# The last pair of output tiles by plain products, and an earlier, fixed order for the pair sums of the last chunk

## The chip, the cores and the metric

The kernel runs on one core of one Trainium2 chip, in one launch. The metric is the device time of an execution in microseconds (us); the lower, the better. Three runs of the kernel before the change took 675.46, 675.48 and 680.38 us, median 675.48.

## The reference

Two stages: a block-sorted attention, and on its output a mixture of 8 experts with a balanced (Sinkhorn) gate. The change lies in the second alone.

```python
def _moe_ref(x, w_gate, w1, w2):          # x 3072x512, w1 8x512x1024, w2 8x1024x512
    logits = x @ w_gate
    P = np.exp(logits - logits.max())
    for _ in range(8):
        P /= P.sum(1, keepdims=True) + 1e-09
        P /= P.sum(0, keepdims=True) + 1e-09
        P *= N / E
    out = np.zeros((N, D), dtype=np.float32)
    for e in range(E):
        h = np.maximum(x @ w1[e], 0.0)
        ye = h @ w2[e]
        out += P[:, e:e + 1] * ye
    return out
```

Every expert is applied to all 3072 rows, and its result is added with the gate's weight of each row.

## The kernel before

The attention and expert 0 come first. Experts 1 to 7 then run over three chunks of 1024 rows each, which makes 21 chunks (`n` from 1 to 21 in the last loop). A chunk has two steps, and the kernel weaves them: while PE (TensorE) does the output products of chunk n, it does the hidden products of chunk n+1 between them (`ahead`, one `next` after each part of an output). Behind chunk 21 there is no hidden work left to weave in.

Hidden step (`hidden`, matmuls at L653): `h = relu(x @ w1)` in transposed form, into a tile `hT` of 128 x 8 x 1024 bf16 (feature within a block, feature block, row of the chunk). Four units i = 0 to 3; unit i makes the blocks i and 4+i. The 2x2 block product is computed by seven block products instead of eight (the Winograd form of Strassen's method). VectorE (L677, L689, L692) and ScalarE (L695) bring the results from PSUM into `hT`; a tile `h3` (L699) gets one of the differences that the output step needs.

Output step (`output7`, matmuls at L740): the chunk's 8 row tiles of 128 rows are taken in four pairs, i = 0 to 3; tile a = 8p + i and tile b = 8p + 4 + i. There are 84 such pairs in the 21 chunks. A pair's product with `w2` is again a 2x2 block product by seven products, each of four matmuls 128x256. It needs three sums of quarters of `hT` (s1, s2, s4), which GpSimd (POOL) makes into a tile `hs` in `sum_h` (L723), and sums of quarters of `w2` (`w2s`), also made by GpSimd. The seven products accumulate into two PSUM tiles, `u` (256 columns) and `x` (512 columns): after some of them the running sum is read by `gather`, and the next product is added to it.

```python
add(u, hT[:, 4:8, ha], b11, True);   gather(e, a, 0, u)
add(x0, hT[:, 0:4, ha], b21, True)
add(u, s2, t2, False);               gather(e, a, 256, u)
add(x1, s1, t1, False);              gather(e, b, 256, x1)
add(u, s3, t3, False);               gather(e, b, 256, u)
add(x1, s4, b22, False);             gather(e, a, 0, x)
add(u, hT[:, 0:4, hb], t4, False);   gather(e, b, 0, u)
```

`gather` (L705) is one VectorE instruction, out = PSUM x gate weight + out, on a float32 accumulator `osbl` in SBUF. For the last expert each finished row tile is stored to DRAM from the SP queue (`store`, L710; for the very last tile b in two halves, L758 and L768).

Order: each engine runs its instructions in the order of its own queue. Instructions that are passed through `pin` keep the order in which the program makes them; the others are placed by a scheduler. `sum_h` isn't pinned before the change. `sum_h(i, hT, f0, f1)` takes the feature blocks f0 to f1 of a quarter. For pair 0 of a chunk it is called twice: for blocks 0 to 2 during the chunk before (128x384 instructions), and for block 3 (128x128) at the chunk's start, as block 3 comes from the last hidden unit. For pair i+1 it is called as a whole (128x512) while pair i is worked on. The pool `hsp` of `hs` tiles has three buffers, PSUM has five banks under the name `bk` and three under `oacc`. In the last chunk the pairs use some `bk` banks for their accumulators too, as the hidden step no longer needs them.

Of the kernel before, what the change touches and what calls it, by code (L numbers as in the profile page):

```python
# [25 lines left out]
def kernel(  # L26
# [11 lines left out]
    nc = tc.nc  # L38
    B, H, S, D = 4, 8, 768, 64
    NB, BL = 8, 96  # L40
    N, Dm, E, F = 3072, 512, 8, 1024
# [22 lines left out]
    pin = tc.keep_in_program_order  # L64
# [12 lines left out]
    w2t = {}  # L77

    def load_w1(e, f0=0, f1=F):
        if e not in w1t:  # L80
            w1t[e] = wp.tile([128, 4, F], BF16, name="w1e")
        pin(nc.gpsimd.dma_start(
            out=w1t[e][:, :, f0:f1],
            in_=moe_w1[e].rearrange("(kk k) f -> k kk f", k=128)[:, :, f0:f1]))

    def load_w2(e):
        w2t[e] = (wq if e else wcp).tile([128, 8, Dm], BF16, name="w2e")
        for f0, f1 in ((0, 8),) if e else ((0, 4), (4, 8)):
            pin(nc.gpsimd.dma_start(
                out=w2t[e][:, f0:f1],  # L90
                in_=moe_w2[e].rearrange("(fb k) f -> k fb f", k=128)[:, f0:f1]))
# [22 lines left out]
    def acc(t, c=0, n=Dm):  # L114
        return osbl[t // 18][:, t % 18, c:c + n]
# [300 lines left out]
    def sum_w(e):  # L416
        wct[e] = (wcq if e % 2 == 0 else wcp).tile([128, 3, 2, F // 2], BF16, name="wc")
        for kk in range(2):
            a11, a21 = (w1t[e][:, kk, f:f + 512] for f in (0, 512))
            a12, a22 = (w1t[e][:, 2 + kk, f:f + 512] for f in (0, 512))  # L420
            s1, s2, s4 = (wct[e][:, j, kk, :] for j in range(3))
            for a, b, o, c in ((a21, a22, ALU.add, s1), (s1, a11, ALU.subtract, s2),
                               (a11, a21, ALU.subtract, a21), (a12, s2, ALU.subtract, s4)):
                pin(nc.gpsimd.tensor_tensor(out=c, in0=a, in1=b, op=o))
                yield

    with tc.tile_pool(name="ps0", bufs=4, space=bass.MemoryType.PSUM,
# [58 lines left out]
        for x in ("s00 k2 s01 k3 p s02 s03 s10 m00 s11 m01 s12 m02 s13 m03 t00 m10 m11 t01 m12 "  # L486
                  "h00 m13 h01 t10 h02 t11 h03 v0 v1 v2 v3 h10").split():
            n = [int(c) for c in x[1:]]
# [29 lines left out]
    with ExitStack() as c2:  # L518
# [53 lines left out]
        for _ in ex:  # L572
# [12 lines left out]
    op = ctx.enter_context(tc.tile_pool(name="op", bufs=3, space=bass.MemoryType.PSUM,  # L585
                                        reuse_waits="tile"))
# [3 lines left out]
    def bank():  # L590
        return bk.tile([128, 512], F32, name="bk")
# [3 lines left out]
    def sum_w2(e):  # L595
        w2s[e] = (w2q.tile([128, 4, 4, Dm // 2], BF16, name="w2s") if e % 2 else
                  wcp.tile([128, 4, 4, Dm // 2], BF16, name="w2e"))
        for k in (0, 2):
            b11, b12 = (w2t[e][:, 4 + k:6 + k, d:d + 256] for d in (0, 256))
            b21, b22 = (w2t[e][:, k:k + 2, d:d + 256] for d in (0, 256))  # L600
            t1, t2, t3, t4 = (w2s[e][:, j, k:k + 2, :] for j in range(4))
            for a, b, c in ((b12, b11, t1), (b22, t1, t2), (b22, b12, t3), (b21, t2, t4)):
                pin(nc.gpsimd.tensor_tensor(out=c, in0=a, in1=b, op=ALU.subtract))
                yield
# [98 lines left out]
    def gather(e, t, c, ps):  # L703
        o = acc(t, c, ps.shape[-1])
        nc.vector.scalar_tensor_tensor(out=o, in0=ps, scalar=glog[:, t, e:e + 1], in1=o,  # L705
                                       op0=ALU.mult, op1=ALU.add)

    def store(e, t):
        if e == E - 1:
            nc.sync.dma_start(out=out[t * 128:(t + 1) * 128, :], in_=acc(t))  # L710

    hs = {}

    def sum_h(i, hT, f0=0, f1=4):

        if f0 == 0:
            hs[i] = hsp.tile([128, 3, 4, 128], BF16, name="hs")
        s1, s2, s4 = (hs[i][:, j, f0:f1] for j in range(3))
        a11, a21, a12, a22 = (hT[:, f + f0:f + f1, t + 128 * i:t + 128 * i + 128]
                              for f in (4, 0) for t in (0, 512))  # L720
        for a, b, o, c in ((a21, a22, ALU.add, s1), (s1, a11, ALU.subtract, s2),
                           (a12, s2, ALU.subtract, s4)):
            nc.gpsimd.tensor_tensor(out=c, in0=a, in1=b, op=o)  # L723

    def output7(e, p, i, hT):
        a, b = 8 * p + i, 8 * p + 4 + i
        ha, hb = slice(128 * i, 128 * i + 128), slice(512 + 128 * i, 640 + 128 * i)
        s1, s2, s4 = (hs[i][:, j] for j in range(3))
        s3 = h3[e, p][:, :, ha]
        t1, t2, t3, t4 = (w2s[e][:, j] for j in range(4))  # L730
        obank = lambda: op.tile([128, Dm], F32, name="oacc")
        last = e == E - 1 and p == 2
        u = (bank if last and i % 2 else obank)()[:, 0:256]
        x = (bank if last and i else obank)()
        x0, x1 = x[:, 0:256], x[:, 256:512]
        b11, b21, b22 = w2t[e][:, 4:8, 0:256], w2t[e][:, 0:4, 0:256], w2t[e][:, 0:4, 256:512]

        def add(ps, h, w, first):
            for fb in range(4):
                nc.tensor.matmul(ps, h[:, fb, :], w[:, fb, :], start=(first and fb == 0),  # L740
                                 stop=(fb == 3), skip_group_check=True)

        add(u, hT[:, 4:8, ha], b11, True)
        gather(e, a, 0, u)
        yield

        add(x0, hT[:, 0:4, ha], b21, True)
        yield
        add(u, s2, t2, False)
        gather(e, a, 256, u)  # L750
        yield
        add(x1, s1, t1, False)
        gather(e, b, 256, x1)
        yield
        add(u, s3, t3, False)
        gather(e, b, 256, u)
        if last and i == 3:
            nc.sync.dma_start(out=out[b * 128:(b + 1) * 128, 256:512],  # L758
                              in_=acc(b, 256, 256))
        yield  # L760
        add(x1, s4, b22, False)
        gather(e, a, 0, x)
        store(e, a)
        yield
        add(u, hT[:, 0:4, hb], t4, False)
        gather(e, b, 0, u)
        if last and i == 3:
            nc.sync.dma_start(out=out[b * 128:(b + 1) * 128, 0:256], in_=acc(b, 0, 256))  # L768
        else:
            store(e, b)  # L770
        yield

    def scale0(ts):
        for t in ts:
            nc.scalar.activation(out=acc(t), in_=acc(t), func=AF.Copy,
                                 scale=glog[:, t, 0:1])
# [7 lines left out]
    def sums(n):  # L784
        while n and queue:
            if next(queue[0], 0) is None:
                n -= 1
            else:
                queue.pop(0)
# [14 lines left out]
    for n in range(56):  # L804
        next(tail0)
        if n == 28:
            hT = htp.tile([128, 8, 1024], BF16, name="hT")
            first = units(1, 0, hT, pin)
        if first:
            next(first)  # L810
            if n == 28 + 21:
                sum_h(0, hT, 0, 3)
        if n in works:
            next(works[n], 0)
        if n in (0, 2, 4, 6, 8, 11, 13, 15, 17, 20, 22, 24, 26, 29, 31, 33, 35, 37, 39):
            next(chain)
        if n == 40:
            pin(nc.gpsimd.tensor_copy(held, glog[0:96, NT - 1, 0:2]))
            sums(8)

    hTs = {0: hT}
# [9 lines left out]
    for n in range(1, 3 * (E - 1) + 1):  # L831
        e, p, hT = 1 + (n - 1) // 3, (n - 1) % 3, hTs[n - 1]
        d = 2 + n // 3
        fetch = n == 1 or n % 3 == 0 and d < E
        if fetch:
            load_w1(d)
            queue.append(sum_w(d))
        for i in range(4):
            if e == 1:
                scale0([t for t in (8 * p + i, 8 * p + 4 + i) if t < 18])  # L840
            if i == 0:
                sum_h(0, hT, 3)
            if i < 3:
                sum_h(i + 1, hT)
            elif n < 3 * (E - 1):
                sum_h(0, hTs[n], 0, 3)
            sums(1 + i // 2)
            for _ in output7(e, p, i, hT):
                next(ahead, 0)
        if fetch:  # L850
            load_w2(d)
            queue.append(sum_w2(d))
# [30 lines left out]
```

## Time and profile before

| What | Value |
|---|---|
| median of 3 runs | 675.48 us |
| the profiled execution's own time | 675.74 us |
| its span, first to last instruction | 673.5 us |
| PE busy | 660.1 us, 98% |
| DVE (VectorE) busy | 544.3 us, 81% |
| POOL (GpSimd) busy | 473.0 us, 70% |
| ACT (ScalarE) busy | 296.1 us, 44% |
| chain that ended last | PE 73%, DVE 1%, POOL 1% |
| L705 gathers into osbl from oacc | 490, mean 521 ns |
| L723 pair sums | 3 x 105, mean 959 ns (all shapes) |

A span is counted from the first to the last instruction of the profiled execution; around it lie 2.2 us of its own time. The profiler's page cuts the span in 40 slices; the views used below (the chain of waits, the timeline of one engine, the stretches) take single microseconds of it, counted from the span's start. A matmul's record is longer than the time to the next one's start, since matmuls are pipelined: the price of one in a stream is read from starts, not from durations.

### The profile page before, as it was taken

The page shows a single profiled execution, that of the slowest core. Times are in us where ns is not written, and L with a number is a line of the kernel's source. Part 1 is how long each engine was busy: PE and PEld are TensorE (multiplying, and loading weights), DVE is VectorE, ACT ScalarE, POOL GpSimd, SP SyncE. Part 2 cuts the span into 40 slices and gives each one's busy share as a digit, 9 for nine tenths or more (in the row PEclk, how much of TensorE's full clock was granted, in tenths as well). Part 3 has the DMA queues.
Part 4 walks back from the last instruction along what each step waited for, and adds up shares of the span by engine and source line. Part 5 has one row for each costly group of instructions (what it writes and reads, how often), then busy time and mean ns, then how long its engine had stood idle before and what let it go on. Part 6 is the DMA issues. An engine that isn't in the chain of part 4 may idle for free.

```text
span 673.5 us, 13293 instructions
## 1 busy us (share of the span) xinstructions
PE 660.1 (98%) x5150; PEld 435.3 (65%) x5150; DVE 544.3 (81%) x1134; ACT 296.1 (44%) x530; POOL 473.0 (70%) x500
## 2 busy tenths in 40 slices
PE   8999999999999999999999999999999999999996
PEld 3656665554666666666666666666666666666675
DVE  6548777663889888888888888988888888888896
ACT  5773863479443434333333334343433334333430
POOL 4713344017897998898897998689886999636745
PEclk9999999999999999999999999999999999999999
DMA  9997964003040340031203040034003220001223
GB/s 158 189 215 133 142 113 64 1 0 54 11 64 6 59 63 1 1 63 29 36 1 63 2 63 1 6 58 63 1 1 65 27 38 1 1 1 62 95 79 142
DMA packets 32800, 36.57 MB, mean 54 GB/s; under 512 B 2097, under 2 KB 25777, under 8 KB 32737
## 3 DMA queue, kind: packets, MB, share of 16 engines
q0 software_dynamic: 26848, 27.57, 26.0%
q1 hardware_dynamic: 5888, 8.15, 3.8%
q8 instruction: 40, 0.66, 0.4%
q14 instruction: 24, 0.19, 0.1%
HBM read 52.45 MB, written 6.29 MB: 87 GB/s over the span
## 4 chain that ended last, share of the span: by engine, by line
PE 73%; DVE 1%; POOL 1%; issue 0%; ACT 0%; DVEq 0%
PE oacc L740 36%; PE bk L653 36%; PE bk L740 1%; DVE osbl L705 1%; POOL hs L723 1%; DVE hT L689 0%; DVE hT L692 0%; ACT p L673 0%; DVEq L705 0%
## 5 line engine op out<-in xcount | busy, mean ns | idle before, releaser
L705 DVE SCALAR_TENSOR_TENSOR osbl<-oacc,glog,osbl 128x256 f32<-128x256 f32 (+1 forms) x490 | 255.2, 521 | 61.6 <-PE oacc L740 61.4
L653 PE MATMUL bk<-xtT,w1e 128*128 128x512 bf16 x504 | 149.7, 379 | 0.0
L723 POOL TENSOR_TENSOR hs<-hT 128x512 bf16<-128x512 bf16 (+2 forms) x105 | 99.4, 959 | 67.6 <-DVE hT L692 67.5
L740 PEld LDWEIGHTS <-hT 128*128 128x128 bf16 x1008 | 98.6, 98 | 64.5 <-issue 1.3
L740 PEld LDWEIGHTS <-hs 128*128 128x128 bf16 x1008 | 98.5, 98 | 64.5 <-POOL hs L723 1.5
L740 PE MATMUL oacc<-w2e,hT 128*128 128x256 bf16 x796 | 119.6, 273 | 0.5 <-ACT hT L695 0.5
L695 ACT ACTIVATE hT<-bk 128x512 bf16<-128x512 f32 x84 | 50.3, 598 | 158.7 <-PE bk L653 158.7
L723 POOL TENSOR_TENSOR hs<-hT,hs 128x512 bf16<-128x512 bf16 (+2 forms) x105 | 99.8, 958 | 4.9
L723 POOL TENSOR_TENSOR hs<-hs,hT 128x512 bf16<-128x512 bf16 (+2 forms) x105 | 99.9, 960 | 4.3 <-ACT hT L695 0.4
L653 PE MATMUL bk<-xc,wc 128*128 128x512 bf16 x336 | 99.9, 379 | 0.2 <-ACT p L673 0.2
L740 PE MATMUL oacc<-w2e,hs 128*128 128x256 bf16 x612 | 92.0, 273 | 0.9 <-POOL hs L723 0.9
L681 ACT COPY u<-bk 128x512 f32<-128x512 f32 x84 | 49.2, 586 | 95.2 <-PE bk L653 94.5
L653 PEld LDWEIGHTS <-w1e 128*128 128x128 bf16 x672 | 65.7, 98 | 10.5
L689 DVE CUSTOM_DVE_ANT_0 hT<-bk,p 128x512 bf16<-128x512 f32 x84 | 58.1, 692 | 11.8 <-ACT p L686 6.4
L699 DVE SCALAR_TENSOR_TENSOR h<-bk,hT 128x512 bf16<-128x512 f32 x84 | 57.1, 680 | 5.8 <-ACT hT L695 5.8
L686 ACT COPY p<-bk 128x512 f32<-128x512 f32 x84 | 49.2, 586 | 23.5 <-PE bk L653 23.5
L673 ACT COPY p<-bk 128x512 f32<-128x512 f32 x84 | 49.3, 587 | 20.1 <-PE bk L653 20.1
L677 DVE CUSTOM_DVE_ANT_0 hT<-bk,p 128x512 bf16<-128x512 f32 x84 | 57.0, 679 | 1.0 <-ACT hT L393 0.6
L692 DVE CUSTOM_DVE_ANT_0 hT<-bk,u 128x512 bf16<-128x512 f32 x84 | 57.1, 679 | 1.0 <-PE bk L653 1.0
L740 PE MATMUL oacc<-w2s,hs 128*128 128x256 bf16 x364 | 54.8, 273 | 0.1
L653 PEld LDWEIGHTS <-wc 128*128 128x128 bf16 x504 | 49.3, 98 | 8.0 <-issue 0.4
L653 PE MATMUL bk<-xtT,wc 128*128 128x512 bf16 x168 | 50.0, 379 | 0.0
(142 smaller groups left out, 838.7 us busy)
## 6 DMA issues: line engine op xcount, KB each, us to landing
w1e<-in_moe_w_dram POOLq DMA_DIRECT2D x7, 1024.0 KB, 8.0
w2e<-in_moe_w_dram POOLq DMA_DIRECT2D x7, 1024.0 KB, 8.8
out_dram<-osbl SPq DMA_DIRECT2D x23, 256.0 KB, 2.0
kvq<-in_v_dram POOLq DMA_DIRECT2D x3, 768.0 KB, 8.5
kvq<-in_k_dram POOLq DMA_DIRECT2D x3, 768.0 KB, 11.1
vsb<-vs SPq DMA_DIRECT2D x17, 97.5 KB, 4.8
kvq<-in_q_dram POOLq DMA_DIRECT2D x4, 384.0 KB, 8.6
kvq<-in_q_dram POOLq DMA_DIRECT2D x2, 768.0 KB, 19.2
```

Source lines behind the costliest of these rows:

```text
L653: hold(nc.tensor.matmul(ps, wa[:, kk, :], xa[:, kk, :], start=(first and kk == 0), stop=(kk == 1), skip_group_check=True))
L673: nc.scalar.copy(p1, u)
L677: nc.vector._custom_dve(TENSOR_ADD_SAT, out=c11, in0=w, in1=p1, s0=TOP, s1=0.0)
L681: nc.scalar.copy(u2, u)
L686: nc.scalar.copy(p5, v)
L689: nc.vector._custom_dve(TENSOR_ADD_SAT, out=c22, in0=u, in1=p5, s0=TOP, s1=0.0)
L692: nc.vector._custom_dve(TENSOR_ADD_SAT, out=c12, in0=v, in1=u2, s0=TOP, s1=0.0)
L695: nc.scalar.activation(out=c21, in_=u, func=AF.Relu)
L699: nc.vector.scalar_tensor_tensor(out=h3[e, p][:, i, :], in0=u, scalar=0.0, in1=c22, op0=ALU.max, op1=ALU.subtract)
L705: nc.vector.scalar_tensor_tensor(out=o, in0=ps, scalar=glog[:, t, e:e + 1], in1=o, op0=ALU.mult, op1=ALU.add)
L723: nc.gpsimd.tensor_tensor(out=c, in0=a, in1=b, op=o)
L740: nc.tensor.matmul(ps, h[:, fb, :], w[:, fb, :], start=(first and fb == 0), stop=(fb == 3), skip_group_check=True)
```

## The change

The last pair (i = 3 of chunk 21) no longer goes through `output7` but through a new `output8`: tile a and then tile b by plain products over all 8 feature blocks, tile a in one PSUM bank of 512 columns, tile b in two of 256 columns, each with one gather and one store. It needs no pair sums, so `sum_h` isn't called for pair 3 of the last chunk.

The pair sums of pair 1 of the last chunk are made in two parts like those of pair 0: blocks 0 to 2 during chunk 20, block 3 at the start of chunk 21. In chunk 21 all pair sums are pinned in program order: block 3 of pair 0, block 3 of pair 1, then pair 2 as a whole.

On all engines the instructions up to the pair sums for chunk 21 stand as before.

```diff
-    def sum_h(i, hT, f0=0, f1=4):
+    def sum_h(i, hT, f0=0, f1=4, hold=lambda ins: ins):
...
-            nc.gpsimd.tensor_tensor(out=c, in0=a, in1=b, op=o)
+            hold(nc.gpsimd.tensor_tensor(out=c, in0=a, in1=b, op=o))
...
         gather(e, b, 256, u)
-        if last and i == 3:
-            nc.sync.dma_start(out=out[b * 128:(b + 1) * 128, 256:512],
-                              in_=acc(b, 256, 256))
...
         gather(e, b, 0, u)
-        if last and i == 3:
-            nc.sync.dma_start(out=out[b * 128:(b + 1) * 128, 0:256], in_=acc(b, 0, 256))
-        else:
-            store(e, b)
-        yield
+        store(e, b)
+        yield
+
+    def output8(e, p, i, hT):
+        for t, c in ((8 * p + i, 128 * i), (8 * p + 4 + i, 512 + 128 * i)):
+            for d, n in ((0, 512),) if t % 8 < 4 else ((0, 256), (256, 256)):
+                ps = bank()[:, 0:n]
+                for fb in range(8):
+                    nc.tensor.matmul(ps, hT[:, fb, c:c + 128], w2t[e][:, fb, d:d + n],
+                                     start=(fb == 0), stop=(fb == 7))
+                gather(e, t, d, ps)
+                nc.sync.dma_start(out=out[t * 128:(t + 1) * 128, d:d + n], in_=acc(t, d, n))
+                yield
...
+            end = n == 3 * (E - 1)
+            hold = pin if end else lambda ins: ins
             if i == 0:
-                sum_h(0, hT, 3)
-            if i < 3:
-                sum_h(i + 1, hT)
-            elif n < 3 * (E - 1):
+                sum_h(0, hT, 3, hold=hold)
+            if i < 3 - end:
+                sum_h(i + 1, hT, 3 if end and i == 0 else 0, hold=hold)
+            elif i == 3 and not end:
                 sum_h(0, hTs[n], 0, 3)
+                if n == 3 * (E - 1) - 1:
+                    sum_h(1, hTs[n], 0, 3)
             sums(1 + i // 2)
-            for _ in output7(e, p, i, hT):
+            for _ in (output8 if end and i == 3 else output7)(e, p, i, hT):
                 next(ahead, 0)
```

## The prediction

> **What bounds the kernel now.** I read the page first, then the chain that ended last in order of time, then the timelines of the engines over the last 25 us, then the stretches at the end. The page says that TensorE (PE) is busy nearly without a break in all of the 40 slices but the outermost ones, so almost everywhere a matmul fewer is worth its length and a wait elsewhere is worth nothing. The diff leaves every engine's instructions as they are up to the last chunk of the last expert, so only the end is to be read closely. There the chain leaves PE:
>
> ```profile
> 650.87 0.43 PE bk L653 x2
> 651.30 0.45 PE oacc L740 x4
> ...
> 655.56 3.04 POOL hs L723 x4
> ...
> 658.93 0.44 PE bk L740 x4
> ...
> 664.65 0.45 PE oacc L740 x4
> ...
> 665.13 2.06 DVE osbl L705 x4
> ...
> 667.23 0.61 PE bk L740 x4
> ...
> 667.87 0.49 DVE osbl L705
> ...
> 668.46 1.15 DVE osbl L705 x2
> ...
> 669.65 0.61 PE bk L740 x4
> ...
> 670.29 0.48 DVE osbl L705
> ```
>
> Columns are start, length, engine, tile, line. Two things are to be seen. The first two lines are the price list: two 128x512 matmuls in 0.43 us and four 128x256 ones in 0.44 us, that is 0.216 and 0.109 us from start to start when nothing waits. And there are two places where PE isn't the chain: GpSimd's pair sums around 655.6 to 658.6 (first pair of the last chunk), and VectorE's gathers from 665.1 on (last pair). The timeline of PE, and that of GpSimd, give the first place its size:
>
> ```profile
> 656.61 0.83 PE L740 MATMUL oacc<-w2s,hs 128*128 128x256 bf16 x4
> 657.28 0.49 PE L740 MATMUL oacc<-w2e,hs 128*128 128x256 bf16 x3
> 658.65 0.28 PE L740 MATMUL oacc<-w2e,hs 128*128 128x256 bf16 x1 [0.88 <-POOL hs L723]
> ```
>
> ```profile
> 649.96 0.91 POOL L723 TENSOR_TENSOR hs<-hT,hs 128x384 bf16<-128x384 bf16 x1
> 654.06 2.65 POOL L723 TENSOR_TENSOR hs<-hT 128x128 bf16<-128x128 bf16 x3 [3.19 <-DVE hT L692]
> 656.67 1.54 POOL L723 TENSOR_TENSOR hs<-hs,hT 128x128 bf16<-128x128 bf16 x2
> ```
>
> GpSimd stands idle for 3.19 us before 654.06, then runs one 128x128 sum (0.43 us) for pair 0, then the two first 128x512 sums of pairs 1 and 2 (1.15 us each) before the second sum of pair 0, and another 128x512 one before its third. PE needs that second sum for the fourth matmul of its group: the third began at 656.83, so it was due at 656.94 and came at 657.16 (0.22 lost). It needs the third sum for the matmul due at 657.49 + 0.11 = 657.60, which came at 658.65 (1.05 lost).
>
> The second place, in PE's timeline again:
>
> ```profile
> 667.23 0.60 PE L740 MATMUL bk<-w2s,hs 128*128 128x256 bf16 x4 [0.20 <-DVE osbl L705]
> 669.65 0.60 PE L740 MATMUL bk<-w2s,hT 128*128 128x256 bf16 x4 [0.65 <-DVE osbl L705]
> ```
>
> With nothing woven in behind it, the last pair's seven products go through two accumulators, each of which must be gathered before the next product is added. By the 0.11 spacing the last groups but two, but one and the last were due at 666.87, 668.10 and 668.84 and came at 667.23, 668.41 and 669.65: 0.37 + 0.30 + 0.81 = 1.48 us lost.
>
> **The change part by part.** First the sums. The changed program's order on GpSimd is six 128x384 sums (pairs 0 and 1 in turn), then three 128x128 of pair 0, three of pair 1, three 128x512 of pair 2; the three 128x512 of pair 3 are gone. The first 128x384 sum starts at 647.99 as before; sums that don't need each other start 0.04 before the last one ends, so six at 0.91 end near 653.25, inside the idle stretch, 0.8 us before VectorE's eviction (L692) lets the next begin at 654.06. Pair 1's new first sum takes the buffer of an older tile whose last matmul started at 647.99 and is done by 648.3, earlier than GpSimd gets to it: no wait. From 654.06: pair 0 at 654.06, 654.60 (it waits for ScalarE's eviction L695, done 654.54), 655.10, ending 655.53; pair 1's three end at 656.92; pair 2's at 660.5. The deadlines by PE's order, with all lost time taken out: pair 0 at 656.94 and 657.37 (1.8 us to spare), pair 1 near 658.6, pair 2 near 662.0 and 663.7 (over 2.5 us to spare). Queued behind a late sum is only the next sum. So the 0.22 + 1.05 = 1.27 us go, and nothing on GpSimd takes their place.
>
> Then the plain products. Removed: 28 matmuls of 128x256, 28 x 0.109 = 3.05 us, with 1.48 us of waits. Added: 8 of 128x512 and 16 of 128x256, 8 x 0.216 + 16 x 0.109 = 3.47 us, in three banks of their own, so no group waits for a gather. Net 0.42 - 1.48 = -1.06 us. VectorE has three gathers (one 128x512 of 0.75, two 128x256 of 0.48) for six, all but the last under PE; the last matmul, the last 128x256 gather and the last 128 KB store are of the same shapes as before, so the 0.31 us from matmul to gather, the 0.48 and the 2.7 us from the issue of the last store (670.80) to the end of the span (673.5) stay. The changed order has one new wait, of PE on its own earlier work, before the third bank: it is for a matmul of pair 1, some 6 us older, and I take 0; were it for the matmul just ahead, it would cost that matmul's 0.27 less the 0.11 it takes anyway and 0.05 of signalling, 0.2. Small waits of PE between (0.08, 0.04, 0.15, 0.08 from 660.3 to 665.7) are rewritten but not removed; going through VectorE's order by hand they come out within 0.1 in sum.
>
> The 128x512 price is where a rule and the rows differ. Rows: 0.216 us from start to start. The Trainium skill (TensorE: Matmul & The Clock Gate, section Back-to-back issue gap) gives a stream of weight loads and matmuls a sustained spacing of about 131 ns at 512 columns. The trace does not bear this out; by it the eight would be 0.7 us shorter, an estimate from that page.
>
> Sum: 1.27 + 1.06 = 2.33 us off. The profiled execution took 675.74 (span 673.5, so 2.24 around it): 673.41. It lies 0.26 above the median of the runs; from 675.48 the same sum gives 673.15, which I round to 673.2. Bounds: the sums' part is worth 0 to 1.27, the plain products' part 0.85 (new wait, at 0.2) to 1.15 (small waits).
>
> **The rivals.**
> 1. *The pair sums stay late.* If the six 128x384 sums slid, through the older buffer or an eviction, past 654.06 by the 1.8 us to spare, pair 0's last part would be as late as now and only the plain products would pay: 675.48 - 1.06 = 674.4. For it: GpSimd has only 0.8 us of idle time left before 654.06. Against: each of the six inputs is there by 648.9.
> 2. *The stores set the end.* Five stores (1.05 MB) now fall within 3.3 us. The stretches of the trace show two rates:
>
> ```profile
> 667.10:668.75 1.65, 1.38 (x12) 1.08 (x12) 1.25 (x4) 0.00 (x0) 0.00 (x0) 1.00 0.84 318
> 670.80:672.20 1.40, 0.00 (x0) 0.00 (x0) 0.00 (x0) 0.00 (x0) 0.00 (x0) 0.86 0.57 195
> ```
>
> The last column is GB/s. At 318 all are through in time. At 195 throughout, 5.4 us from about 666.0 end at 671.4, where the last packets now end at 672.1: the gain shrinks to 0.7, 674.8. Against: 195 is the rate of the two small last stores, which move no faster because they are issued 0.7 apart.
> 3. *The three added sums block VectorE* (the slower side). They now run at 649 to 653, beside VectorE's evictions for the last hidden tiles, where GpSimd stood idle. If each held VectorE off for its whole 0.91 us, and PE waited for those evictions, 3 x 0.91 = 2.73 us come back: 675.48 - 2.33 + 2.73 = 675.9. It decides from 0.78 us per sum on. Against it: the gathers at 655.64 to 656.9 lie under GpSimd's sums and take 0.474 each, the one at 652.92 under none and takes 0.474. The Trainium skill (SBUF — State Buffer, section Who interferes with whom) says that VectorE contends with GpSimd when it has two inputs in SBUF; the gathers and evictions have one there and one in PSUM, and the equal durations agree.
> 4. *128x512 matmuls are cheaper in this stream.* If they overlapped so that eight took 0.7 us less, 672.5. Against: the chain lists them in pairs at 0.43 us all along the chunks before.
>
> **How the numbers follow.** The forecast has 0.78, rival 1 0.09, rival 2 0.07, rival 3 0.04, rival 4 0.02. The forecast's own range, from the unknown costs above and the 0.26 between the profiled and the median run, is 672.7 to 673.8. For 8 in 10 with the first two rivals partly taken in: 672.4 to 675.0. Faster or slower by over 1% (6.8 us, about what a measurement of this kernel can tell from no change) lies outside every case: 0.97 within 1%, 0.01 faster, 0.02 slower.
>
> **What would show it.** In the changed profile: six 128x384 sums back to back from 648 to 653.3; no wait of PE's for GpSimd in the last 20 us; no wait of PE's for VectorE over 0.2 us in the last 5; the last 24 matmuls without a break but for the groups of pair 2 woven in; the last store issued near 668.5 and 2.7 us behind it. The prediction is wrong if the last matmul starts later than 668.3, if the stretch after the last store's issue grows, or if anything before 647 has moved.

## The result, and the profile after

The changed kernel takes 673.31 us (median of 22 runs), the kernel before 675.66 (22 runs): 2.35 us less. The ratio is 0.9963, 95% interval [0.995, 0.9976]. The forecast was 2.33 us less, 673.2 us. It was counted from the 675.48 of three runs; from the 675.66 of these 22 the same gain gives 673.33.

Both kernels have a few executions that are 3 to 5 us longer, which makes the interval wide, and the profiled execution of the change is one of them: 676.73 us, with a span of 674.5. Its stretches show where. The column behind the engines' busy times is the granted clock:

```profile
17.00:34.00 17.00, 16.16 (x207) 11.99 (x202) 9.28 (x19) 10.02 (x14) 12.70 (x19) 0.80 1.09 187
26.00:29.00 3.00, 3.00 (x35) 2.71 (x34) 1.78 (x4) 1.08 (x2) 3.00 (x5) 0.50 1.31 203
```

In the attention stage, far ahead of the change, the clock averages 0.80 over these 17 us; from 26 to 29 us it is 0.50. In the profile of before it is 1.00 there. All that follows comes 3.29 us later than before up to the last eviction of the hidden step (the step that brings a result from PSUM to SBUF), and has nothing to do with the edit. The lines of after are therefore from a second profile (called *again* below: 673.47 us, span 671.2, clock 1.00 in these stretches). From 551 to 654 us its instructions start within 0.02 us of those in the profile of before, so that the two can be read against each other by the clock on the wall. That the two match so well is chance: another execution of the changed kernel (again_b) reaches the last eviction 0.28 us earlier. GpSimd's timeline, again, and below it the line of before for pair 0's third sum:

```profile
647.98 1.78 POOL L723 TENSOR_TENSOR hs<-hT 128x384 bf16<-128x384 bf16 x2 [6.52 <-DVE hT L692]
649.72 1.78 POOL L723 TENSOR_TENSOR hs<-hs,hT 128x384 bf16<-128x384 bf16 x2
651.46 1.78 POOL L723 TENSOR_TENSOR hs<-hT,hs 128x384 bf16<-128x384 bf16 x2
654.06 0.43 POOL L723 TENSOR_TENSOR hs<-hT 128x128 bf16<-128x128 bf16 x1 [0.82 <-DVE hT L692]
654.67 0.43 POOL L723 TENSOR_TENSOR hs<-hs,hT 128x128 bf16<-128x128 bf16 x1 [0.18 <-ACT hT L695]
655.18 0.42 POOL L723 TENSOR_TENSOR hs<-hT,hs 128x128 bf16<-128x128 bf16 x1
```

```profile
658.17 1.54 POOL L723 TENSOR_TENSOR hs<-hT,hs 128x128 bf16<-128x128 bf16 x2
```

The idle stretch of 3.19 us before 654.06 has become 0.82: six sums where there were three. Pair 0's third sum, which started at 658.17 before, now starts at 655.18. PE's timeline, again:

```profile
656.61 0.60 PE L740 MATMUL oacc<-w2s,hs 128*128 128x256 bf16 x4
657.04 0.60 PE L740 MATMUL oacc<-w2e,hs 128*128 128x256 bf16 x4
...
664.92 2.99 PE L772 MATMUL bk<-w2e,hT 128*128 128x512 bf16 x21
```

Both groups of pair 0 are whole and 0.43 apart; before, the second broke off for 0.88 us. The last row holds 5 matmuls of 128x512 and 16 of 128x256 in one piece, where the last twenty matmuls of before have three waits among them. The chain of waits, again, ends on PE and one gather:

```profile
664.56 0.52 PE oacc L740 x4
665.08 2.84 PE bk L772 x21
667.92 0.03 issue
667.95 0.48 DVE osbl L705
```

It has no piece of GpSimd's left, and one of VectorE's, the last. 21 matmuls in 2.84 us is the price list of before to 0.02 us: 5 x 0.216 + 16 x 0.109 = 2.82.

### The profile page after: what moved, and what is told of

Its sections match the earlier page's. It is cut to its first block, busy times and chain, and to the rows that moved or that the text cites. A ratio compares the mean times of both kernels' runs of the same rounds, so it can differ in the third digit from the quotient of the medians.

```text
span 674.5 us, 13204 instructions
## 1 busy us (share of the span) xinstructions
PE 658.7 (98%) x5069; PEld 437.2 (65%) x5146; DVE 542.8 (80%) x1131; ACT 296.1 (44%) x530; POOL 469.7 (70%) x500
## 4 chain that ended last, share of the span: by engine, by line
PE 73%; issue 0%; DVE 0%; ACT 0%
PE oacc L740 38%; PE bk L653 34%; PE bk L740 1%; PE bk L772 1%; DVE osbl L705 0%; ACT p L673 0%
## 5 line engine op out<-in xcount | busy, mean ns | idle before, releaser
L653 PE MATMUL bk<-xtT,w1e 128*128 128x512 bf16 x475 | 143.5, 379 | 0.9
L695 ACT ACTIVATE hT<-bk 128x512 bf16<-128x512 f32 x84 | 50.3, 598 | 158.7 <-PE bk L653 140.9
L653 PE MATMUL bk<-xc,wc 128*128 128x512 bf16 x319 | 96.3, 379 | 0.6 <-ACT p L673 0.2
L689 DVE CUSTOM_DVE_ANT_0 hT<-bk,p 128x512 bf16<-128x512 f32 x84 | 58.1, 691 | 11.8 <-ACT p L686 6.4
L692 DVE CUSTOM_DVE_ANT_0 hT<-bk,u 128x512 bf16<-128x512 f32 x84 | 57.0, 679 | 1.0 <-PE bk L653 1.0
L653 PE MATMUL bk<-xtT,wc 128*128 128x512 bf16 x159 | 48.0, 379 | 0.0
```

Source lines behind the costliest of these rows:

```text
L653: hold(nc.tensor.matmul(ps, wa[:, kk, :], xa[:, kk, :], start=(first and kk == 0), stop=(kk == 1), skip_group_check=True))
L689: nc.vector._custom_dve(TENSOR_ADD_SAT, out=c22, in0=u, in1=p5, s0=TOP, s1=0.0)
L692: nc.vector._custom_dve(TENSOR_ADD_SAT, out=c12, in0=v, in1=u2, s0=TOP, s1=0.0)
L695: nc.scalar.activation(out=c21, in_=u, func=AF.Relu)
```

## The experiments

Eleven runs were made, two of them of the changed kernel itself (again, again_b). To take out what differs between executions ahead of the change, two places are counted from the end of the last eviction of the hidden step (L695, at 653.94 + 0.60 in the trace of before; executions of one kernel reach it at times that differ by 0.3 us): the start of the last matmul and the issue of the last store. "Lower" is the difference of the median to that of before, measured beside it (675.57 to 675.76).

| Kernel | last matmul, us | last store, us | median, us | lower, us | ratio to before, 95% |
|---|---|---|---|---|---|
| before | 15.44 | 16.26 | 675.66 | | |
| changed (again) | 13.11 | 13.93 | 673.34 | 2.42 | 0.9962 [0.9937, 0.9987] |
| changed (again_b) | 13.10 | 13.93 | 673.44 | 2.15 | 0.9968 [0.9942, 0.9994] |
| sums_only | 14.15 | 14.97 | 674.37 | 1.20 | 0.9988 [0.9976, 0.9999] |
| plain_only | 14.40 | 15.22 | 674.43 | 1.14 | 0.9994 [0.9978, 1.0009] |
| pin_only | 14.37 | 15.19 | 674.72 | 0.85 | 1.0001 [0.9985, 1.0017] |
| ahead_only | 14.15 | 14.97 | 674.57 | 1.00 | 0.9996 [0.9981, 1.0012] |
| no_pin | 13.10 | 13.93 | 673.46 | 2.13 | 0.9965 [0.994, 0.999] |
| all_plain | 13.89 | 14.72 | 673.80 | 1.96 | 0.9967 [0.9953, 0.9982] |
| b_whole | 12.98 | 14.17 | 673.87 | 1.89 | 0.9961 [0.9936, 0.9985] |
| two_queues | 13.10 | 13.93 | 673.79 | 1.97 | 0.9962 [0.9944, 0.998] |
| woven | 12.94 | 13.99 | 674.08 | 1.51 | 0.9973 [0.9949, 0.9996] |

Of the kernels that keep one part of the change, the ratio alone parts only sums_only from no change, and barely; nor does it part the variants from each other. The medians do only roughly (the changed kernel's own three medians are 673.31, 673.34 and 673.44, and a kernel's median and its last store differ by up to 0.4 us). What parts them is the place and size of each wait in the traces, counted from that eviction: they agree to 0.01 us between executions.

**The sums alone.** Seven products for the last pair too, with pair 3's sums pinned behind pair 2's.

```diff
-            if i < 3 - end:
+            if i < 3:
...
-            for _ in (output8 if end and i == 3 else output7)(e, p, i, hT):
+            for _ in output7(e, p, i, hT):
```

The diff is against the changed kernel; the last tile's store in two halves is that of before.

> Both changes to the pair sums of the last chunk, all four pairs by seven products as before. Theory (the change is two gains that add: 1.27 us from the sums, 1.06 us from the plain products): 1.27 us under the kernel before, no wait of PE's for GpSimd in the last 20 us, the three waits for VectorE in the last pair (0.37, 0.30, 0.81 us) still there. Rival (the plain products bring it all, and the end is set by the last pair whatever the sums do): no change.

Measured 1.20 us less by the median, 1.29 by the last matmul. No wait for GpSimd is left in the last chunk. The timeline of PE of this run keeps the waits of the last pair:

```profile
665.66 0.60 PE L740 MATMUL bk<-w2s,hs 128*128 128x256 bf16 x4 [0.20 <-DVE osbl L705]
668.08 0.60 PE L740 MATMUL bk<-w2s,hT 128*128 128x256 bf16 x4 [0.65 <-DVE osbl L705]
```

They are the two lines of before, 0.20 and 0.65, moved to an earlier time. The rival is out.

**The plain products alone.**

```diff
-            hold = pin if end else lambda ins: ins
+            hold = lambda ins: ins
...
-                sum_h(i + 1, hT, 3 if end and i == 0 else 0, hold=hold)
+                sum_h(i + 1, hT, 0, hold=hold)
...
-                if n == 3 * (E - 1) - 1:
-                    sum_h(1, hTs[n], 0, 3)
```

> Only the last pair by plain products, the pair sums as before. Theory: 1.06 us under the kernel before, the two waits of PE's for GpSimd (0.22 and 1.05 us) still there. Rival (the sums bring it all, the plain products' 0.42 us of extra matmuls and their saved waits cancel): no change.

Measured 1.14 us less, 1.04 by the last matmul. PE's timeline here still has the break of 0.88 us in pair 0:

```profile
658.46 0.28 PE L740 MATMUL oacc<-w2e,hs 128*128 128x256 bf16 x1 [0.88 <-POOL hs L723]
```

So the halves are 1.29 and 1.04, and they add: 2.33, which is what the two together give by the last matmul (15.44 - 13.11). In the one half PE waits for GpSimd, in the other for VectorE, at different times, and neither wait hides the other.

**Which part of the sums' edit does it.** Two runs with one part each, seven products everywhere. In pin_only pair 1's sums are made whole in the last chunk, as before, and the last chunk's sums are pinned; in ahead_only pair 1's blocks 0 to 2 are made in chunk 20, and nothing is pinned. The diffs are against sums_only:

```diff
 pin_only:
-                sum_h(i + 1, hT, 3 if end and i == 0 else 0, hold=hold)
+                sum_h(i + 1, hT, 0, hold=hold)
...
-                if n == 3 * (E - 1) - 1:
-                    sum_h(1, hTs[n], 0, 3)
 ahead_only:
-            hold = pin if end else lambda ins: ins
+            hold = lambda ins: ins
```

> Half of the sums' part: program order alone, pair 1's sums whole at the start of the last chunk as before; seven products everywhere. By the rows of before pair 0's sums end at 655.5 (due 656.9), pair 1's second sum at 657.9 against a due time of 657.8, pair 2's and 3's in time: 1.15 us under the kernel before, a wait of about 0.1 us left. Rival (the order is worth nothing without the earlier start): no change, PE waits over 1 us for the sums of pair 1.

> The other half: pair 1's first three blocks a chunk ahead, no program order kept; seven products everywhere. GpSimd's order then has one 128x512 sum of pair 2 between pair 0's first and second 128x128 sum: by the rows pair 0's second ends at 656.4 (due 656.9) and its third at 657.1 (due 657.4): 1.27 us under the kernel before, as much as both together, so that the two halves are each enough. Rival (the order is what counts): PE still waits for GpSimd, less than half of the gain.

In pin_only PE's one wait for GpSimd is before pair 1's second sum, 0.21 us (0.1 expected; GpSimd began pair 0's second sum 0.08 late, behind ScalarE's eviction, and the two steps behind it moved with it). PE's timeline of pin_only has it:

```profile
657.20 0.49 PE L740 MATMUL bk<-w2e,hT 128*128 128x256 bf16 x3
657.74 0.28 PE L740 MATMUL bk<-w2s,hs 128*128 128x256 bf16 x1
```

Three matmuls from 657.20 on, 0.109 apart, make the next one due at 657.53; it came at 657.74. The last matmul comes 1.07 us earlier than before (1.15 expected). In ahead_only no wait for GpSimd is left, and the last matmul comes 1.29 us earlier, exactly as with both. The medians, 0.85 and 1.00 lower, fall short of that by 0.2 to 0.3 us. GpSimd's timeline of ahead_only shows why the order doesn't matter there:

```profile
654.33 1.92 POOL L723 TENSOR_TENSOR hs<-hT 128x128 bf16<-128x128 bf16 x3 [0.81 <-DVE hT L692]
656.20 0.81 POOL L723 TENSOR_TENSOR hs<-hs,hT 128x128 bf16<-128x128 bf16 x2
656.98 0.81 POOL L723 TENSOR_TENSOR hs<-hT,hs 128x128 bf16<-128x128 bf16 x2
```

The scheduler still puts a 128x512 sum of pair 2 into the first group, but only one, and the sums of pair 1 between pair 0's are 128x128. This execution runs 0.26 us later than that of before, so the second and third sum of pair 0 end at 656.37 and 657.14 on the clock of before, due at 656.94 and 657.37. The earlier start is enough by itself, the order nearly so.

**The earlier start without the order, in the changed kernel.**

```diff
-            hold = pin if end else lambda ins: ins
+            hold = lambda ins: ins
```

> The changed kernel without the program order of the sums: only the earlier start of pair 1's sums, and the plain products. If the earlier start alone is enough, as in the kernel without plain products: the same place of the last matmul and the same time as the changed kernel, 673.3 us. If the two need each other once the last pair is shorter: up to 1.3 us more.

The last matmul and the last store stand at the same places as in the changed kernel, and beside it the medians are 673.46 and 673.44. In the changed kernel the program order is worth nothing once the earlier start is made.

**The price of plain products, four times over.**

```diff
-            if i == 0:
+            if i == 0 and not end:
                 sum_h(0, hT, 3, hold=hold)
...
-            for _ in (output8 if end and i == 3 else output7)(e, p, i, hT):
+            for _ in (output8 if end else output7)(e, p, i, hT):
```

The other calls of `sum_h` for chunk 21 are left out in the same way.

> All four pairs of the last chunk by plain products, no pair sums for that chunk. Theory (a 128x512 matmul costs 0.216 us, a plain pair 0.42 us more than seven products): 3 x 0.42 = 1.27 us more than the changed kernel, less up to 0.4 us of small waits for gathers in pairs 0 to 2: 0.8 to 1.2 us more, 674.1 to 674.5. Rival (512 columns in a stream cost about 0.13 us, by the spacing that the Trainium skill gives): a plain pair is 0.26 us cheaper than seven products, and this kernel some 1.5 us faster than the changed one.

A miss in the time: 0.46 us more than the changed kernel, below the 0.8 expected. By the last matmul it is 0.79 more. The chain of this run has all but the first plain matmul in one piece:

```profile
654.72 13.69 PE bk L772 x95
```

31 x 0.216 + 64 x 0.109 = 13.67 us. So the spacing of 128x512 matmuls in this stream of weight loads and matmuls is 0.216 us. The sum of the small waits in the last chunk, with the one just ahead of it, falls from 0.51 to 0.04, and 3 x 0.42 - 0.47 = 0.79. The sustained spacing of about 131 ns at 512 columns that the Trainium skill gives (TensorE: Matmul & The Clock Gate, section Back-to-back issue gap) does not hold here: by it the 95 would have taken 11.0 us, an estimate from that page.

The median lies 0.3 us below what the place of the last matmul says. From the start of the last matmul to the end of the execution's own time it is 5.64 us in the profile of all_plain and 5.83 in again; but it is 5.54 in plain_only, which ends in the same instructions as the changed kernel. This stretch varies by 0.3 us without an edit; what makes it vary is open.

**What lies behind the last matmul.** Two variants of the end.

```diff
 b_whole:
-            for d, n in ((0, 512),) if t % 8 < 4 else ((0, 256), (256, 256)):
+            for d, n in ((0, 512),):
 two_queues (the very last store only):
-                nc.sync.dma_start(out=out[t * 128:(t + 1) * 128, d:d + n], in_=acc(t, d, n))
+                for eng, r in ((nc.sync, 0), (nc.scalar, 64)):
+                    eng.dma_start(out=out[t * 128 + r:t * 128 + r + 64, d:d + n],
+                                  in_=acc(t, d, n)[r:r + 64])
```

> The very last row tile in one bank of 512 columns with one gather and one 256 KB store, in place of two halves. Theory (the end is last matmul, gather, store in a row): the matmuls cost the same, the gather starts 0.11 us later behind its matmul and takes 0.75 in place of 0.48, the store takes 0.2 to 0.3 longer: 0.6 us slower than the changed kernel. Rival (the store's fixed time is all that counts behind the last matmul): 0.4 slower or less.

> The last 128 KB store as two of 64 partitions, one from SP's queue and one from ScalarE's, issued at the same time. If the transfer of the 1 KB packets (0.5 us in the trace of before) is limited by its one queue: 0.2 us faster than the changed kernel. If it is the fixed time from issue to first packet (0.8) and from last packet to the end (1.4) that counts: no change, or a little slower for the second issue.

b_whole is 0.53 us slower than the changed kernel (0.6 expected, 0.4 or less for the rival). The parts: last matmul 0.13 earlier, the 0.75 us gather, so that the store is issued 0.25 later, and from its issue to its last packet 1.65 us against 1.41. Matmul, gather and store are in a row, as the theory has it. two_queues is 0.45 slower: no gain, and far more than the "little slower" of the second side. The two rows of the issuing queues, SP's and ScalarE's timelines of this run:

```profile
668.26 0.55 SPq L780 DMA_DIRECT2D out_dram<-osbl  x1
```

```profile
668.26 0.57 ACTq L780 DMA_DIRECT2D out_dram<-osbl  x1
```

In again the last issue takes 0.33 us; here the two take 0.55 and 0.57. By the packets of the two traces, the first one comes 1.20 (SP) and 1.49 us (ScalarE) behind the issue in place of 0.80, and the last one ends 1.93 us behind it in place of 1.41. So the time went into the start of the transfers. Whether the shared moment does this, or something else about the second queue, no run here shows.

**Filling the small waits.** Only some 0.36 us of PE's lost time is left in pairs 0 to 2. In this kernel `output8` yields after each matmul, and steps of pairs 1 and 2 pull it along:

```diff
+                    if fb < 7:
+                        yield
...
+            if end and i == 0:
+                ahead = output8(e, p, 3, hT)
-            for _ in (output8 if end and i == 3 else output7)(e, p, i, hT):
-                next(ahead, 0)
+            for k, _ in enumerate(ahead if end and i == 3 else output7(e, p, i, hT)):
+                if not end or 0 < i < 3 and k < 6:
+                    next(ahead, 0)
```

> The changed kernel with the last pair's plain products begun earlier: one of their matmuls after each of the first six steps of pairs 1 and 2, so that they lie under PE's four small waits for gathers (0.085, 0.038, 0.154, 0.086 us in the changed kernel's trace). Theory (those waits are all that is left of PE's lost time in the last chunk, and any matmul that needs no gather fills them): no wait of PE's over 0.05 us in the last 13 us, last matmul 0.36 us earlier than in the changed kernel, 672.9 to 673.1 us. Rival (VectorE becomes the limit, as the same gathers now come with a 128x512 one between them): waits of the same size elsewhere, no change.

A miss: 0.64 us slower than the changed kernel beside it (674.08 to 673.44). Of the first three waits 0.02 us is left, but the fourth stays (0.08, in pair 2), a new one of 0.09 comes up ahead of it, and the last matmul is 0.16 us earlier, not 0.36. And the stores now set the end. SP's timeline of woven, and below it that of again:

```profile
666.40 0.81 SPq L710 DMA_DIRECT2D out_dram<-osbl  x2
667.75 0.84 SPq L777 DMA_DIRECT2D out_dram<-osbl  x2
```

```profile
665.16 0.81 SPq L710 DMA_DIRECT2D out_dram<-osbl  x2
666.98 1.81 SPq L775 DMA_DIRECT2D out_dram<-osbl  x3
```

With the last pair's work brought forward, pair 2 ends later, and the first of its two 256 KB stores is issued 1.35 us ahead of the first of the two 128 KB ones (666.40 and 667.75); in the changed kernel it is 2.70 us (665.16 and 667.86, the second of the three). By the traces the last three stores, one of 256 KB and two of 128 KB, land 2.67, 2.44 and 2.31 us behind their issues; in again the three of the same sizes take 2.11, 1.98 and 1.74. The last packet ends 1.87 us behind the last issue, in place of 1.41. That is the kind of loss that the prediction's second rival has, at a spacing that the change itself doesn't reach. That the spacing alone makes it is read from this one trace; no run changed only the spacing.

## Why the prediction was right

**Reading the last 20 us alone.** Right. From 551 to 654 us the instructions of again start within 0.02 us of those of before, so that the whole difference between these two profiles was to be found in two places of the chain.

**The sums' term, 1.27.** Measured 1.29. The six sums end at 653.24 (653.25 said), pair 0's third at 655.60 (655.53 said; its second waited 0.07 longer behind ScalarE's eviction). What the prediction took as one step are two, one of which is enough: the earlier start gives 1.29 by itself, the order 1.07. The step did not ask this, since both were made together; the deadlines that it worked out had 1.8 us to spare for that reason.

**The plain products' term, 1.06.** Measured 1.04. The price of a matmul by starts, 0.216 and 0.109, held for the new stream. The new wait of PE's for its own older matmul cost nothing, as taken: the 21 matmuls run through it. The small waits for gathers came out at 0.51 with the one ahead of the chunk, unchanged (0.50 before). The 1.48 us of waits is right; of the three groups named as "last but two, but one and the last", the first, at 667.23, is the last but three.

**The end.** By the sum the last matmul moves from 669.98 to 667.65; the store was forecast "near 668.5". They came at 667.64 and 668.46, and the span ended 2.78 us behind the store (2.7 said).

**The rivals.** Sums late: out, no wait for GpSimd is left. Stores: not in the change. The kind of loss shows in woven, at 0.46 us between issue and last packet where the rival priced 1.6, and it needs stores closer than the change puts them. Blocking of VectorE: out. Beside the added sums, again has 0.485 and 0.478 for the gathers at 651.77 and 652.91 and 0.692 for L689 at 652.30; before, without sums beside them, it was 0.485, 0.474 and 0.691: at most 0.004 us each. (L692, at 653.30, starts behind the last of the six.) Cheaper 128x512: out by all_plain.

## What to carry to other kernels

At the end of a kernel, where nothing is left to weave in, the algorithm with fewer products can lose to the plain one: here 0.42 us more matmuls bought off 1.48 us of waits, once; done for all four pairs it cost more than it saved. Helper work for the next stage belongs into the idle stretch ahead of its last input, cut so that only the part which needs that input is left; here the order of the queue mattered only where that wasn't done. Work brought forward at the end pushes other work's stores back: price the last stores' spacing together with the matmuls.

## What the runs showed that was not expected

The last store split over two queues and issued at the same moment was slower than one store from one queue: the issues took 0.55 and 0.57 us against 0.33, and the last packet came 0.5 us later, though each moved only 64 KB. The last matmul of woven came 0.16 us earlier than that of the changed kernel, and the kernel took 0.64 us longer.
